# Two neighbouring tokens per partition, and the heads in two halves, in a gated-linear-attention plus feed-forward kernel

## Chip, cores, metric

The kernel runs on one core of one Trainium2 chip. The metric is device time in microseconds (us). "Span" is the length of the profiled execution as the profile shows it, 1.7 to 2.9 us shorter than the time of the same run. Runs are marked fast or slow (over 1.5% above the fastest of the same kernel); ratios use fast runs alone.

Engines: PE multiplies matrices, DVE, ACT and POOL work on vectors, and SP does nothing but issue DMAs, one after the other, in the order in which the program has them. "SPq" in the profile is SP's instruction queue.

## The reference, cut to what matters

```python
# q, k, v, alpha: (B=4, H=8, S=768, D=48) float32
for t in range(S):
    state = alpha[:, :, t, :, None] * state + einsum('bhd,bhe->bhde', k[:, :, t], v[:, :, t])
    y[:, :, t] = einsum('bhd,bhde->bhe', q[:, :, t], state)
x = y.transpose(0, 2, 1, 3).reshape(3072, 384)
g = s * relu(x @ w_in) ** 2 + b          # w_in: 384 x 2048
out = g @ w_out                          # w_out: 2048 x 384
```

One caution about "correct": the constant `b` times the column sums of `w_out` makes up nearly all of the output. With the reference's own numbers, max |out| is 0.236, and max |out - bias| is 0.0020. A correctness check on `out` therefore says little of the attention part.

## The kernel before

The 3072 tokens are 24 blocks of 128. Attention is computed block by block in chunk form: cumulative sums of log alpha on PE, exponentials on ACT, q and k scaled on DVE, q and k transposed, then k^T v, the masked q k^T, and y. Block for block, y is transposed and goes through the two feed-forward layers, called MoE here as in the parameters' names. The order of all instructions is fixed beforehand by a list scheduler inside the kernel, which is given an estimated duration for each operation (the second argument of `op`).

For each block there are four loads, the store of 128 output rows, and DMA transposes for those blocks that PE does not transpose:

```python
NIN = 9              # buffers per input tensor: loads run up to 9 blocks ahead
N_PE_T = 12          # blocks 0..11 are transposed by PE, 12..23 by DMA
...
a_in = many("a_in", NIN, [128, H, D], FP32)      # one token per partition; q_in, k_in, v_in too

def load(n, src, dst):
    b, c = n // NCH, n % NCH
    nc.sync.dma_start(
        out=dst[n % NIN],
        in_=src[b, :, c * C : (c + 1) * C, :].rearrange("h s d -> s h d"),
    )                                            # 1024 pieces of 48 floats = 192 bytes

def st_Tdma(n):                                  # q and k of a block, one DMA
    nc.sync.dma_start_transpose(
        out=qkT_sb[n % 3].rearrange("a x p t -> a (x p) t"),
        in_=qk_sb[n % 3].rearrange("a x h d -> a (x h d)"),
    )

def ostore(x):
    n = x // 4
    nc.sync.dma_start(out=out[n * C : (n + 1) * C, :], in_=out_sb[(x // 4) % NOUT])
...
op("SP", 0.45, ranks[x, n], load, n, src, dst, w=[(x, n % NIN)], lat=1.2, dma=0.98)
op("SP", 0.5, -3000, st_Tdma, n, r=[("qb", i3), ("kb", i3)], w=[("qkT", i3)], lat=TLAT, dma=1.6)
```

The bias needs column sums of `w_out`, which POOL adds up early on:

```python
def colsum_part(i):
    nc.gpsimd.tensor_tensor(out=colpart if i else colsum,
        in0=wst[i][:, 0 : QW // 2], in1=wst[i][:, QW // 2 : QW], op=ALU.add)
...
op("POOL", 1.3, -2, colsum_part, i, r=[("wst", i)], w=["colpart" if i else "colsum"])
op("PE", 1.3, -10, bias_mm, r=["bones", "colsum"], w=["bps"], lat=0.27, take=("b", 0))
```

## Time and profile before

| | before |
|---|---|
| time, median of 4 runs | 202.02 us (201.06 to 204.6; the 204.6 is a slow run) |
| span of the profiled run | 198.0 us, clock 0.974, fast |
| PE busy | 173.1 us, 87% of the span |
| DMAs issued by SP (its timeline) | 148 |
| last input load issued | 148.5 us |
| last q/k transpose issued | 151.5 us |

A table of stretches of the kernel before. The columns are the stretch, its length, busy us of PE, PEld, DVE, ACT and POOL with their instruction counts, the granted PE clock, the mean busy share of the 16 DMA engines, and GB/s:

```profile
0.00:50.00 50.00, 31.25 (x323) 23.90 (x324) 27.36 (x43) 25.30 (x52) 26.14 (x41) 0.91 1.02 217
60.00:120.00 60.00, 58.23 (x691) 39.88 (x689) 50.48 (x85) 44.56 (x106) 25.31 (x35) 1.00 0.97 192
```

Some of that seems to be back-pressure: a load issue takes from 0.37 us to over 4 us, the long ones where the DMA engines are full. How much of the 89% is the bare cost of an issue, and how much is waiting for a saturated DMA, can't be read off; only the shortest issues hint at it (0.37 to 0.44 us for a load, 1.24 us for a q/k transpose, 0.33 us for a store).

### The profile page before, as it was taken

The numbers are of one execution on the slowest core, as the hardware profiler recorded it, in microseconds if no ns is written. First come the engines' busy times: TensorE is split into PE (matmuls) and PEld (weight loads), VectorE is DVE, ScalarE is ACT, GpSimd is POOL, SyncE is SP. The second block draws the span as 40 slices with busy tenths as digits, with TensorE's granted clock in tenths as the row PEclk, the third lists the DMA queues.
The fourth block names the chain that finished last, engine by engine and source line by source line (L and its number), as shares of the span: only waits on it lengthen the run. The fifth ranks groups of instructions, "written<-read, shape, count | busy, mean of one in ns | idle before, by whom it ended". The sixth has DMA issues, their size and how long they took to land.

```text
span 198.0 us, 4422 instructions
## 1 busy us (share of the span) xinstructions
PE 173.1 (87%) x1664; PEld 111.3 (56%) x1664; DVE 130.1 (66%) x223; ACT 114.1 (58%) x249; POOL 66.2 (33%) x97
## 2 busy tenths in 40 slices
PE   0557279985999999799999999999999999999991
PEld 0445279652778877576555564555564455455650
DVE  4545626268999999988986935896664672653321
ACT  3415307993558967778767847796336661944000
POOL 6515044996823544606154333232233000000000
PEclk9999958998899999999999999999999999999999
DMA  6998999999397989899999997989997420111112
GB/s 115 193 219 173 180 322 372 197 212 206 98 218 172 218 187 209 157 219 186 238 136 201 219 191 164 217 173 192 196 184 196 100 63 4 40 40 41 69 60 75
DMA packets 124982, 32.94 MB, mean 166 GB/s; under 512 B 118304, under 2 KB 124960, under 8 KB 124960
## 3 DMA queue, kind: packets, MB, share of 16 engines
q1 hardware_dynamic: 123072, 31.08, 73.7%
q0 software_dynamic: 1600, 1.57, 5.2%
q8 instruction: 13, 0.21, 0.4%
q14 instruction: 9, 0.07, 0.1%
q10 hardware_dynamic: 288, 0.00, 0.1%
HBM read 25.17 MB, written 4.72 MB: 151 GB/s over the span
## 4 chain that ended last, share of the span: by engine, by line
PE 62%; SPq 11%; DVE 8%; POOL 6%; DMA 6%; issue 3%; ACT 1%; DVEq 0%; POOLq 0%
PE bank L531 25%; PE bank L559 24%; SPq L274 9%; DMA v_in<-in_v_dram 4%; POOL colsum L309 3%; POOL colpart L301 3%; DMA k_in<-in_k_dram 3%; PE a_ps L446 3%; PE bank L382 2%; DVE am L455 2%; PE bank L479 2%; PE bank L405 1%; DVE qk L370 1%; DVE gt L552 1%; PE bank L338 1%
## 5 line engine op out<-in xcount | busy, mean ns | idle before, releaser
L540 ACT ACTIVATE r<-bank 128x512 bf16<-128x512 f32 x96 | 56.2, 602 | 34.6 <-PE bank L531 18.1
L531 PE MATMUL bank<-xd,w_in_bf 128*128 128x128 bf16 (+2 forms) x480 | 75.2, 303 | 0.8 <-DMA w_in_bf<-in_moe_w_in_dram 0.5
L559 PE MATMUL bank<-w_out_bf,gt 128*128 128x384 bf16 x384 | 71.9, 328 | 0.6 <-ACT w_out_bf L298 0.5
L552 DVE TENSOR_TENSOR gt<-r 128x512 bf16<-128x512 bf16 x96 | 48.4, 520 | 25.3 <-ACT r L540 24.9
L531 PEld LDWEIGHTS <-w_in_bf 128*128 128x128 bf16 x480 | 39.8, 103 | 20.4 <-DMA w_in_bf<-in_moe_w_in_dram 0.7
L559 PEld LDWEIGHTS <-gt 128*128 128x128 bf16 x384 | 36.0, 98 | 25.9 <-issue 2.0
L455 DVE TENSOR_TENSOR am<-a_ps,mask 128x1024 bf16<-128x1024 f32 x24 | 29.2, 1219 | 5.1 <-PE a_ps L446 4.9
L435 POOL TENSOR_TENSOR s_st<-t,blast 64x192 bf16<-64x192 bf16 x32 | 18.5, 579 | 35.3 <-DVE t L428 14.7
L359 POOL CAST vb<-v_in 128x384 bf16<-128x384 f32 x24 | 15.4, 642 | 32.6 <-DMA v_in<-in_v_dram 26.5
L331 ACT ACTIVATE la<-a_in 128x384 bf16<-128x384 f32 x24 | 12.7, 531 | 11.7 <-DMA a_in<-in_alpha_dram 11.7
L362 DVE TENSOR_TENSOR qk<-q_in,b_s 128x384 bf16<-128x384 f32 x24 | 15.7, 656 | 4.9 <-ACT b_s L352 4.8
L370 DVE TENSOR_TENSOR qk<-k_in,binv 128x384 bf16<-128x384 f32 x24 | 15.9, 664 | 3.5 <-DMA k_in<-in_k_dram 3.5
L352 ACT ACTIVATE b_s<-bank 128x384 f32<-128x384 f32 x24 | 11.8, 492 | 9.1 <-PE bank L343 8.8
L591 POOL TENSOR_TENSOR o_sb<-o_sb,bias_w 128x384 f32<-128x384 f32 x12 | 12.5, 1043 | 12.2 <-ACT o_sb L582 9.8
L568 DVE SCALAR_TENSOR_TENSOR o_sb<-bank,s_col,bias_w 128x384 f32<-128x384 f32 x12 | 7.4, 615 | 13.6 <-PE bank L559 13.6
L492 ACT ACTIVATE yn<-bank 128x384 bf16<-128x384 f32 x24 | 11.9, 497 | 5.8 <-PE bank L479 5.6
L428 DVE TENSOR_TENSOR t<-bank,s_st 128x384 bf16<-128x384 f32 x16 | 8.8, 551 | 7.0 <-PE bank L405 5.0
L338 PE MATMUL bank<-la,U_bf 128*128 128x384 bf16 x24 | 8.2, 340 | 5.0 <-POOL bones L313 4.7
L405 PE MATMUL bank<-vb,qk 128*128 128x96 bf16 x80 | 7.3, 218 | 5.4 <-POOL vb L359 4.1
L355 ACT ACTIVATE binv<-bank 128x384 f32<-128x384 f32 x24 | 11.8, 490 | 0.0
L479 PE MATMUL bank<-vb,am 128*128 128x48 bf16 x192 | 9.0, 186 | 3.0 <-DVE am L455 2.8
L382 PE MATMUL bank<-ident_bf,qk 128*128 128x128 bf16 x96 | 9.9, 250 | 1.6 <-DVE qk L362 1.2
(44 smaller groups left out, 130.7 us busy)
## 6 DMA issues: line engine op xcount, KB each, us to landing
a_in<-in_alpha_dram SPq DMA_DIRECT2D x24, 192.0 KB, 3.6
q_in<-in_q_dram SPq DMA_DIRECT2D x24, 192.0 KB, 3.7
k_in<-in_k_dram SPq DMA_DIRECT2D x24, 192.0 KB, 3.8
v_in<-in_v_dram SPq DMA_DIRECT2D x24, 192.0 KB, 4.0
out_dram<-o_sb SPq DMA_DIRECT2D x24, 192.0 KB, 2.4
wst<-in_moe_w_out_dram SPq DMA_DIRECT2D x4, 768.0 KB, 10.1
w_in_bf<-in_moe_w_in_dram POOLq DMA_DIRECT2D x4, 384.0 KB, 7.0
qkT<-qk SPq DMA_TRANSPOSE x12, 3.6
```

Of the source, the lines that this page charges most:

```text
L274: nc.sync.dma_start(out=dst[n % NIN], in_=src[b, :, c * C : (c + 1) * C, :].rearrange("h s d -> s h d"),)
L359: nc.gpsimd.tensor_copy(out=vb_sb[n % 3], in_=v_in[n % NIN])
L362: nc.vector.tensor_tensor(out=qk_sb[n % 3][:, 0, :, 0:D], in0=q_in[n % NIN], in1=b_sb[n % 2], op=ALU.mult,)
L370: nc.vector.tensor_tensor(out=qk_sb[n % 3][:, 1, :, 0:D], in0=k_in[n % NIN], in1=binv_sb[n % 2], op=ALU.mult,)
L382: nc.tensor.transpose(out=t_ps[:, x, p, :], in_=f[:, 128 * p : 128 * p + 128], identity=ident_bf,)
L435: nc.gpsimd.tensor_tensor(out=s_sb[n % 2][rows, :, cols], in0=t1_sb[n % 2][rows, :, cols], in1=blast_sb[n % 2][rows].unsqueeze(2).to_broad ...
L455: nc.vector.tensor_tensor(out=am_sb[n % 2].rearrange("a e p t -> a (e p) t"), in0=a_ps.rearrange("a e p t -> a (e p) t"), in1=mask.unsquee ...
L479: nc.tensor.matmul(out=y_ps[:, 48 * h : 48 * h + 48], lhsT=am[:, h % 2, h // 2, :], rhs=vb[:, 48 * h : 48 * h + 48], start=(h == 0 and not ...
L531: nc.tensor.matmul(out=hp[:, i * n : (i + 1) * n], lhsT=w_in_bf[:, kk, 128 * j : 128 * (j + 1)], rhs=xd_sb[g % 3][:, kk, 0:n], start=(kk = ...
L540: nc.scalar.activation(out=r_sb[w % 2], in_=bank("h", w), func=AF.Relu)
L552: nc.vector.tensor_tensor(out=dst, in0=r, in1=r, op=ALU.mult)
L559: nc.tensor.matmul(out=op[:, 0:d_model], lhsT=gt_sb[:, slot, j, :], rhs=w_out_bf[:, j, :], start=(j == 0), stop=(j == NJ - 1),)
```

## The change

The intent: each partition holds two neighbouring tokens of four heads, instead of one token of eight heads. Two neighbouring tokens of one head are contiguous in memory, so the transfers become 384 bytes instead of 192, which should take less DMA time for the same data. Partitions 0 to 63 hold heads 0 to 3, and 64 to 127 hold heads 4 to 7; even and odd tokens are two "slots" in the free dimension. Everything else follows: cumulative sums take three matmuls, q k^T sixteen 64x64 quadrants instead of eight half-array matmuls, and v is stored block-diagonally (zeros elsewhere) so that both halves go through one matmul. As the two halves lie in different partitions and different heads, each load, each q/k transpose and each store becomes two DMAs of half the size.

The change also moves other things: PE transposes q and k only of blocks 0 to 2 instead of 0 to 11, so nine more blocks use DMA transposes; column sums go from POOL to DVE; dummy matmuls keep the PE clock up in the first 36 us; ACT issues half of the loads of blocks 0 to 2. The order of the first loads, the grouping of blocks for the feed-forward layers and the split of the output work between engines change as well.

The diff, cut to its core:

```diff
-NIN = 9
-N_PE_T = 12
+NIN = 8
+N_PE_T = 3
+N_PE_Y = 12
+N_ACT_LOAD = 3
...
-    a_in = many("a_in", NIN, [128, H, D], FP32)
+    a_in = many("a_in", NIN, [128, G, 2, D], FP32)         # G = H // 2
...
-    def load(n, src, dst):
+    def load(eng, n, src, dst, e):
         b, c = n // NCH, n % NCH
-        nc.sync.dma_start(
-            out=dst[n % NIN],
-            in_=src[b, :, c * C : (c + 1) * C, :].rearrange("h s d -> s h d"),
-        )
+        eng.dma_start(                                     # R = C // 2 = 64
+            out=dst[n % NIN][R * e : R * e + R].rearrange("i h t d -> i h (t d)"),
+            in_=src[b, G * e : G * e + G, c * C : (c + 1) * C, :].rearrange(
+                "h (i t) d -> i h (t d)", t=2
+            ),
+        )
...
     def st_Tdma(n):
-        nc.sync.dma_start_transpose(
-            out=qkT_sb[n % 3].rearrange("a x p t -> a (x p) t"),
-            in_=qk_sb[n % 3].rearrange("a x h d -> a (x h d)"),
-        )
+        for g in range(2):
+            nc.sync.dma_start_transpose(
+                out=qkT_sb[n % 3][:, g].rearrange("a x u c -> a (x u) c"),
+                in_=qk_sb[n % 3][R * g : R * g + R].rearrange("a x u e d -> a (x u e d)"),
+            )
...
     def st_A(n):
         qkT = qkT_sb[n % 3]
-        for p in range(NP):
-            for e in range(2):
-                nc.tensor.matmul(
-                    out=a_ps[:, e, p, :],
-                    lhsT=qkT[64 * e : 64 * e + 64, 1, p, :],
-                    rhs=qkT[64 * e : 64 * e + 64, 0, p, :], ...)
+        for t in range(2):
+            for p in range(2):
+                for g in range(2):
+                    for e in range(2):
+                        nc.tensor.matmul(
+                            out=a_ps[R * g : R * g + R, e, p, t, :],
+                            lhsT=qkT[64 * e : 64 * e + 64, g, 1, 2 * t + p],
+                            rhs=qkT[64 * e : 64 * e + 64, g, 0, 2 * p : 2 * p + 2], ...)
...
     def ostore(x):
-        nc.sync.dma_start(out=out[n * C : (n + 1) * C, :], in_=out_sb[(x // 4) % NOUT])
+        for t in range(2):
+            nc.sync.dma_start(
+                out=out[n * C : (n + 1) * C, :].rearrange("(j t) m -> t j m", t=2)[t],
+                in_=out_sb[(x // 4) % NOUT][R * t : R * t + R],
+            )
...
-            op("SP", 0.45, ranks[x, n], load, n, src, dst, w=[(x, n % NIN)], lat=1.2, dma=0.98)
+            for e in range(2):
+                eng = nc.scalar if e and n < N_ACT_LOAD else nc.sync
+                op("ACT" if eng is nc.scalar else "SP", 0.45, ranks[x, n], load, eng, n, src, dst, e,
+                   w=[(x, n % NIN, e)], lat=1.2, dma=0.34)
```

## The prediction

> **What bounds it now.** The table of stretches of time shows PE busy 97 to 100% from 50 to 180 us; the chain of waits gives PE 62% of the span. So the kernel is PE-bound after a bad first 50 us, in which PE did about 24 us of useful work, counted at the warm spacing of its timeline: 13 first-layer and 9 second-layer units at 0.66 us, attention for about 4 blocks, the 2.1 us fp32 bias. The other 26 us are waits and cold clock: 4.7 us before the first matmul; 4.1 us until v of block 2 lands (DMA share about 1 from 5 to 35 us); granted clock 0.50 from 25 to 30 us; 3.0 us waiting for the column sums on POOL (adds of 1.85 us). After 50 us only 3 to 4 us are lost; the tail after the last matmul is 4 us.
>
> **PE work** (warm start-to-start, timeline). Before, per block: cumulative sum 0.27, transposes 0.44 (12 blocks), k^T v 0.17, q k^T 0.33, y 0.47, y transpose 0.17 (12 blocks). After, estimates from the same spacings: sum 0.43 (two more 192-column matmuls), k^T v 0.33 (192 columns for 96), q k^T about 0.5 (sixteen 64x64 quadrants for eight), y 0.54. Transposes on PE fall to 3 blocks (-4.0 us), the bias halves (-1.1). Sum: 164 us before, about 172 after: +8 us on the bounding engine. Least certain is q k^T: the Trainium skill, "TensorEngine Tiling (Array Packing)", Restrictions, says column tiling disables fast weight load; the trace has only 128-column loads (95 ns).
>
> **DMA.** 192-byte packets move 196 GB/s when saturated (15.7 ns a packet on each of 16 engines), 1536-byte ones about 350 (70 ns). A line through both puts 384 bytes at 23 ns: 0.75 us a tensor instead of 1.0. The Trainium skill, "DMA: Bandwidth & Descriptors", Specifications, puts line rate at 512 B and up: a gain, not a doubling. It saves 24 us of DMA in all, 4 us in the first 16 tensors; nine more blocks transposed by DMA spend most of it. After 50 us DMA is not the bound. SP issues twice as many loads; its queue gets fuller (about 150 us), a risk.
>
> **Start.** Twelve load issues stand before the first Ln on ACT (about 0.5 us each), and the POOL prelude grows from 4.7 to about 9 us. So the first Ln comes near 8 us, not 4.2, the first MoE matmul near 17, not 14. But then blocks 1, 2 and 3 are there, dummy matmuls hold the clock, and column sums on DVE don't stop PE: from about 20 us it runs nearly full. Loss before steady state: 14 to 17 us instead of 26.
>
> **Sum.** -10 us at the start, +8 us PE work: a tie by this count; it charges the small matmuls fully, so I lean to a gain: 196.5 us, range 189 to 204. Faster by over 2%: 0.52; within: 0.37; slower: 0.11.
>
> **What would show it.** First MoE matmul at 16 to 18 us; no PE idle over 2 us after 22 us; granted clock 1.0 from 20 us; useful PE work in the first 50 us up from 24 to about 35 us; loads near 290 GB/s when saturated; q k^T 0.45 to 0.6 us a block; PE 97% or more to the end.
>
> **What would break it.** Quadrant matmuls at 0.8 us a block; half-size DMA transposes costing as much as whole ones, or the SP queue, starving attention after 60 us; DVE overloaded at 30 to 50 us by column sums; w_in late because POOL issues it late.

## More of the kernel before

The page of the kernel before: busy time of the engines; then the span in 40 slices of 4.95 us each, with the busy share in tenths (9 is 90% or more); then the chain of work that ended last.

```profile
span 198.0 us, 4422 instructions
PE 173.1 (87%) x1664; PEld 111.3 (56%) x1664; DVE 130.1 (66%) x223; ACT 114.1 (58%) x249; POOL 66.2 (33%) x97
...
PE   0557279985999999799999999999999999999991
...
PEclk9999958998899999999999999999999999999999
DMA  6998999999397989899999997989997420111112
...
PE 62%; SPq 11%; DVE 8%; POOL 6%; DMA 6%; issue 3%; ACT 1%; DVEq 0%; POOLq 0%
```

From about 50 us on (slice 10) PE is at 9 nearly everywhere, and it makes up 62% of the chain. The losses lie in the first slices. But the DMA row stands at 7 to 9 nearly everywhere too, up to slice 30, so two resources run near full side by side.

The timeline of SP in the kernel before; the columns are start, duration, line, and what is issued. L274 is a load, L395 a q/k transpose, L511 a y transpose, L579 a store:

```profile
99.94 0.57 SPq L274 DMA_DIRECT2D a_in<-in_alpha_dram  x1
100.60 1.21 SPq L511 DMA_TRANSPOSE xd<-yn  x1
101.86 0.57 SPq L274 DMA_DIRECT2D q_in<-in_q_dram  x1
...
103.17 2.57 SPq L395 DMA_TRANSPOSE qkT<-qk  x1
105.84 0.53 SPq L579 DMA_DIRECT2D out_dram<-o_sb  x1
```

These durations are the time for which SP is held by one issue.

Between 60 and 148.5 us SP is issuing for 79.2 of 88.5 us, 89%.

## The result, and the profile after

The changed kernel takes 279.93 us (median of 4, 278.48 to 280.57), against 202.02 us before. All its runs are fast ones; of the four before, the 204.6 us run is a slow one and left out of the ratio. The ratio is 1.387, with a 95% interval of 1.377 to 1.397. (A ratio here is the mean time of one kernel's fast runs over that of the other's of the same rounds, so not quite the ratio of the medians quoted beside it.) The prediction, 196.5 us with a range up to 204, was wrong by 83 us.

The page of the kernel after; the slices are now 6.97 us long:

```profile
span 278.8 us, 5424 instructions
PE 208.3 (75%) x2025; PEld 139.9 (50%) x2025; DVE 130.8 (47%) x255; ACT 112.1 (40%) x243; POOL 61.8 (22%) x128
...
PE   4188899295766868496859649749669868999993
...
PEclk9997999868995979777995995986887997999999
DMA  5999976566656666557656668656656556220132
...
PE 36%; DMA 25%; SPq 25%; ACT 4%; issue 3%; DVE 3%; POOL 1%; ACTq 0%; DVEq 0%; POOLq 0%
```

Up to slice 4 (35 us) DMA is full, and PE is busy from slice 2 on (of its work in these 35 us, 6.0 us are the dummy matmuls). After that PE is at 4 to 9, once at 2, with no pattern, for 200 us, and it is not the DMA engines that fill up in its place: they fall from 9 to 5 to 7. In the chain PE's share went from 62 to 36%; SP's queue went from 11 to 25%, and DMA from 6 to 25%.

The same stretches of the kernel after, to set beside those of before:

```profile
0.00:50.00 50.00, 35.95 (x497) 30.00 (x498) 30.82 (x60) 25.47 (x54) 21.45 (x59) 0.97 0.89 202
60.00:120.00 60.00, 40.92 (x497) 30.66 (x496) 26.20 (x49) 23.95 (x58) 16.82 (x26) 0.84 0.63 129
```

From 60 to 120 us PE is busy for 40.9 us instead of 58.2, at a granted clock of 0.84, and DMA moves 129 GB/s at a share of 0.63 instead of 192 at 0.97. What PE waits for is shown by the waits of the kernel after (who waits for what: us in total, times, longest):

```profile
POOL vb L436 <- DMA v_in<-in_v_dram: 93.9, 24, 9.8
ACT la L394 <- DMA a_in<-in_alpha_dram: 64.9, 19, 5.8
...
PE bank L401 <- ACT la L394: 29.6, 16, 6.5
```

The cumulative sums on PE (L401) wait for Ln on ACT (the longest such wait, 6.5 us, is the late start; 17.1 of the 29.6 us fall between 60 and 223 us), and Ln waits 64.9 us in total for alpha to land; before it was 11.7 us. So the inputs come late, although DMA engines are free. The timeline of SP tells why. L325 is a load, L477 a q/k transpose, L669 a store; "x2" is two issues in a row:

```profile
98.78 1.28 SPq L325 DMA_DIRECT2D k_in<-in_k_dram  x2
100.11 1.27 SPq L325 DMA_DIRECT2D v_in<-in_v_dram  x2
101.49 2.54 SPq L477 DMA_TRANSPOSE qkT<-qk  x2
104.12 1.26 SPq L325 DMA_DIRECT2D a_in<-in_alpha_dram  x2
...
106.14 1.20 SPq L669 DMA_DIRECT2D out_dram<-o_sb  x2
```

SP issues almost without a gap (0.05 us between issues). A half load holds it for 0.59 us at least, 0.61 us typically. Here that is hardly back-pressure, since the DMA share is 0.6; and the very first half load of this kernel, with nothing in flight yet, took 0.76 us. A half-size q/k transpose holds it 1.2 us, as long as a whole one did (1.24 us at least before), and a half store 0.58 us. From 60 to 223 us SP is issuing for 149.5 of 163 us, 92%, and the rest is nearly all gaps of under 0.2 us between issues. It issues 286 DMAs instead of 148, and over the whole run its issues take 218 us instead of 145; the last load goes out at 223.7 us instead of 148.5, the last q/k transpose at 234.7 instead of 151.5. The 92% alone would prove nothing, as it was 89% before, with back-pressure in it; what tells is the DMA share beside it, 0.63 here and 0.97 before. The load stream has a ceiling that can be worked out (an estimate): 98,304 bytes per issue of 0.61 us and a gap of 0.05 us is 149 GB/s. In a stretch in which SP issued nothing but loads, the table of the kernel after shows 138 GB/s at a DMA share of 0.62:

```profile
38.00:47.00 9.00, 8.57 (x107) 6.16 (x106) 7.48 (x14) 7.46 (x17) 1.12 (x2) 1.00 0.62 138
```

**Theory.** SP's issue rate is the bound. Cutting each DMA in two nearly doubled the number of issues (18 of the 138 more are the q/k transposes of nine more blocks), and a half does not cost half. Per block that is about 8 x 0.61 + 2 x 1.22 + 2 x 0.58 us, and 1.2 us more for the y transpose of twelve blocks: 8.5 to 9.7 us, while PE needs about 7 us for a block (an estimate: 168 us over 24 blocks, counted at the warm spacings of its timeline).

**Rivals.** (a) The DMA engines handle the 384-byte packets, or the many DMAs, badly. (b) The half-size transposes alone are to blame. (c) The late start: the first MoE matmul comes at 26.5 us instead of 14.0, since ACT issues twelve loads ahead of its first Ln. (d) PE's new matmuls are slow, quadrants above all.

### The profile page after: what moved, and what is told of

It is laid out like the page before. It is cut to its first block, busy times and chain, and to the rows that moved or that the text cites. A ratio compares the mean times of both kernels' runs of the same rounds, so it can differ in the third digit from the quotient of the medians.

```text
span 278.8 us, 5424 instructions
## 1 busy us (share of the span) xinstructions
PE 208.3 (75%) x2025; PEld 139.9 (50%) x2025; DVE 130.8 (47%) x255; ACT 112.1 (40%) x243; POOL 61.8 (22%) x128
## 4 chain that ended last, share of the span: by engine, by line
PE 36%; DMA 25%; SPq 25%; ACT 4%; issue 3%; DVE 3%; POOL 1%; ACTq 0%; DVEq 0%; POOLq 0%
SPq L325 16%; PE bank L620 15%; DMA a_in<-in_alpha_dram 13%; PE bank L648 12%; SPq L477 5%; DMA k_in<-in_k_dram 5%; SPq L669 4%; DMA q_in<-in_q_dram 3%; DMA v_in<-in_v_dram 3%; PE bank L568 2%; ACT la L394 2%; PE bank L401 2%; ACT r L629 1%; PE bank L488 1%; DVE am L540 1%
## 5 line engine op out<-in xcount | busy, mean ns | idle before, releaser
L620 PE MATMUL bank<-xd,w_in_bf 128*128 128x128 bf16 (+2 forms) x576 | 83.1, 296 | 1.3 <-ACT r L629 1.3
L648 PE MATMUL bank<-w_out_bf,gt 128*128 128x384 bf16 x384 | 80.4, 354 | 0.1
L620 PEld LDWEIGHTS <-w_in_bf 128*128 128x128 bf16 x576 | 48.6, 106 | 23.6 <-issue 8.0
L436 POOL CAST vb<-v_in 64x384 bf16<-64x384 f32 x48 | 26.5, 553 | 116.8 <-DMA v_in<-in_v_dram 93.9
L394 ACT ACTIVATE la<-a_in 128x384 bf16<-128x384 f32 x24 | 12.5, 526 | 75.4 <-DMA a_in<-in_alpha_dram 64.9
L444 DVE TENSOR_TENSOR qk<-q_in,b_s 128x192 bf16<-128x192 f32 x48 | 17.5, 406 | 37.6 <-ACT b_s L422 24.3
L401 PE MATMUL bank<-la,U_bf 128*128 128x384 bf16 x24 | 9.5, 395 | 29.6 <-ACT la L394 29.6
L518 POOL TENSOR_TENSOR s_st<-t,blast 64x192 bf16<-64x192 bf16 x32 | 17.6, 549 | 32.5 <-PE bank L557 11.7
L488 PE MATMUL bank<-vb,qk 128*128 128x192 bf16 x80 | 11.6, 275 | 17.4 <-POOL vb L436 17.3
L568 PE MATMUL bank<-vb,am 128*128 128x96 bf16 x192 | 14.8, 231 | 7.9 <-DVE am L540 7.9
L488 PEld LDWEIGHTS <-qk 128*128 128x128 bf16 x80 | 7.6, 108 | 20.3 <-issue 15.3
L568 PEld LDWEIGHTS <-am 128*128 128x128 bf16 x192 | 12.0, 113 | 9.1 <-DVE am L540 8.3
L531 PE MATMUL a_ps<-qkT 64*64 64x128 bf16 x384 | 11.6, 233 | 4.7 <-DMA qkT<-qk 4.6
```

Source lines behind the costliest of these rows:

```text
L394: nc.scalar.activation(out=la_sb[n % 2][:, :, :, 0:D], in_=tokens(a_in[n % NIN]), func=AF.Ln)
L436: nc.gpsimd.tensor_copy(out=vb_sb[n % 3][rows, :, e].rearrange("a t (h d) -> a t h d", h=G), in_=tokens(v_in[n % NIN][rows]),)
L444: nc.vector.tensor_tensor(out=qk_sb[n % 3][:, 0, heads, :, 0:D], in0=tokens(q_in[n % NIN][:, heads]), in1=b_sb[n % 2][:, :, heads], op=ALU ...
L488: nc.tensor.matmul(out=p_ps[:, p], lhsT=kb[:, 2 * t + p], rhs=vb[:, t, :, 96 * p : 96 * p + 96], start=(t == 0), stop=(t == 1),)
L518: nc.gpsimd.tensor_tensor(out=s_sb[n % 2][rows, :, cols], in0=t1_sb[n % 2][rows, :, cols], in1=blast_sb[n % 2][rows].unsqueeze(2).to_broad ...
L568: nc.tensor.matmul(out=y_ps[:, :, 48 * h : 48 * h + 48], lhsT=am[:, e, p, t, :], rhs=vb[:, t, :, 48 * h : 48 * h + 48], start=(h == 0 and ...
```

## The experiments

Thirteen kernels were run. "Ratio" is against the kernel before in the same rounds; its median was between 198.5 and 199.9 us in all of them.

| run | made from | edit | median us | ratio |
|---|---|---|---|---|
| e1_whole_issues | after | one DMA instead of two, everywhere | 209.38 | 1.051 |
| e2_T_on_PE | after | all transposes of q, k on PE | 245.68 | 1.237 |
| e3_loads_two_queues | after | second halves of all loads issued by ACT | 265.47 | 1.335 |
| e4_before_half_loads | before | each load in two DMAs of 64 partitions | 237.52 | 1.195 |
| e5_whole_loads_only | after | one DMA per load only | 228.42 | 1.150 |
| e6_loads_two_queues_late | after | second halves on ACT, not those of blocks 3 to 7 | 259.84 | 1.309 |
| e7_before_colsum_DVE | before | column sums on DVE | 194.25 | 0.981 |
| e8_no_loads_on_ACT | after | no loads on ACT | 283.06 | 1.429 |
| e9_before_loads_by_heads | before | each load in two DMAs of 128 partitions | 217.87 | 1.094 |
| e10_T_on_PE_two_queues | after | e2 and e6 together | 232.57 | 1.171 |
| e11_colsum_and_T_by_DMA | before | e7, and nine more blocks transposed by DMA | 210.21 | 1.060 |
| e12_colsum_and_v2_earlier | before | e7, and other order of first loads | 198.70 | 1.000 |
| e13_late_queue_clean_start | after | e2, and second halves on ACT from block 12 on | 242.35 | 1.215 |

### e1_whole_issues: the changed kernel with whole DMAs

The bytes and the 384-byte packets stay, but each pair of DMAs is one. With the two halves holding different heads, no single DMA could be found that puts the data where the kernel wants it; so this kernel loads, transposes and stores *wrong data* (same amounts, same shapes of packets). Its output is wrong, which doesn't matter for the time.

```diff
 def load(eng, n, src, dst, e):
+    if e: return
+    s0 = min(c * C, S - 2 * C)
-        out=dst[n % NIN][R * e : R * e + R]..., in_=src[b, G * e : G * e + G, c * C : (c + 1) * C, :]...
+        out=dst[n % NIN]..., in_=src[b, 0:G, s0 : s0 + 2 * C, :]...        # 128 partitions, heads 0..3
 # q/k transpose: one of 128 partitions instead of two of 64; store: one of 128 rows; no loads on ACT
```

> The changed kernel with the same bytes, the same 384-byte packets and the same work on every engine, but one issue where it has two: one 128-partition load per tensor and block, one transpose, one store, all on SP. Data are wrong on purpose (each load takes 256 tokens of four heads). Theory SP (the changed kernel is bound by the SP queue, which takes 0.6 us for each half load, 1.22 us for each half transpose, 0.58 us for each half store, about 9.2 us a block): with about 4.5 us a block SP is no longer the limit, the PE is: 195 to 210 us. Rival DMA (the transfers themselves, smaller destination halves or the transposes, are the limit): bytes and packets are the same, so 260 us or more. Rival PE (quadrant matmuls, cold clock): unchanged, 270 to 280 us.

Measured: 209.38 us (207.24 to 211.8), ratio 1.051. That is inside the expected range. The profiled run is the slow one (211.8 us), so its durations and DMA rates are read, not its span. The timeline of SP in e1, where L328 is a load:

```profile
100.97 0.43 SPq L328 DMA_DIRECT2D k_in<-in_k_dram  x1
101.45 0.58 SPq L328 DMA_DIRECT2D v_in<-in_v_dram  x1
...
103.22 0.45 SPq L668 DMA_DIRECT2D out_dram<-o_sb  x1
```

And the same stretches of the table in e1:

```profile
38.00:47.00 9.00, 9.00 (x121) 6.97 (x120) 8.85 (x17) 8.32 (x19) 4.84 (x6) 1.00 1.08 285
60.00:120.00 60.00, 53.77 (x649) 39.01 (x652) 43.63 (x86) 38.73 (x91) 22.41 (x39) 0.91 1.08 233
```

Twice the bytes now go out in about 0.5 us of SP, and the last load is issued at 120.4 us instead of 223.7. 285 GB/s in place of 138 from 38 to 47 us, with the same packets and the same matmuls: that refutes (d) as the cause of the 80 us, and (a) as far as the packets go. Nor do the many DMAs clog the engines: from issue to landing a load took a median of 2.9 to 3.0 us in the kernel after, and 3.6 to 4.0 before. The change cost 38.7% (ratio 1.387); with whole DMAs it costs 5.1%. So 33.6 of the 38.7 points, about 67 us, go with the second issues. Not quite all of it need be theirs: e1 also has no loads on ACT, and its first MoE matmul comes at 19.6 us instead of 26.5, so up to 7 us may be the earlier start. The other 5 points, some 10 us, stay: by the same table DMA is saturated (1.08) from 60 to 120 us, where the loads end, and PE is not full until then. So even with half the issues this change would not have won.

### e5_whole_loads_only: only the loads made whole

e1's edit of the loads alone, again with wrong data.

```diff
 def load(eng, n, src, dst, e):        # as in e1
 # q/k transposes and stores stay in halves
```

> As e1_whole_issues, but only the loads are whole; transposes and stores stay two half issues each. Data wrong on purpose. Theory SP, by addition: the stores and transposes cost 1.2 + 2.5 us a block on SP as before the experiment, the loads 2 us instead of 5.2: about 6 to 7 us a block, near the PE's 7: 212 to 228 us, between e1_whole_issues (209.4) and the changed kernel (280). If the half transposes were the cause and the loads not, it stays above 255.

Measured: 228.42 us (226.88 to 230.41), ratio 1.150, 0.4 us above what was expected. So 23.7 points (1.387 - 1.150, about 47 us, with the same earlier start in it) go with the second issue of each load, and 9.9 points (1.150 - 1.051, about 20 us) with the second transposes and stores. Rival (b) fails: the transposes are the smaller part.

### e4_before_half_loads: the kernel before, with nothing changed but the cut of its loads

The counter-proof, with right data and without any other part of the change.

```diff
 def load(n, src, dst):
-    nc.sync.dma_start(out=dst[n % NIN], in_=src[b, :, c * C : (c + 1) * C, :].rearrange("h s d -> s h d"))
+    for e in range(2):
+        nc.sync.dma_start(
+            out=dst[n % NIN][64 * e : 64 * e + 64],
+            in_=src[b, :, c * C + 64 * e : c * C + 64 * e + 64, :].rearrange("h s d -> s h d"))
```

> The kernel before with each load issued as two loads of 64 partitions on SP; same 192-byte packets, same bytes, right result. Theory SP: eight issues of 0.6 to 0.65 us a block, 5.2 us, plus 1.3 to 3 us of transposes and stores: loads are late and the time rises to 215 to 235 us. Rival DMA or PE: bytes and packets are the same, 200 to 206 us.

Measured: 237.52 us (235.65 to 238.34), ratio 1.195, 2.5 us above the expected range and far from the 200 to 206 us of the rivals. The same 192-byte packets, the same bytes, the same work of PE: 39 us slower for being asked for in two. The timeline of SP in e4:

```profile
0.72 1.52 SPq L275 DMA_DIRECT2D a_in<-in_alpha_dram  x2
...
99.57 1.27 SPq L275 DMA_DIRECT2D a_in<-in_alpha_dram  x2
100.94 1.27 SPq L275 DMA_DIRECT2D q_in<-in_q_dram  x2
102.31 1.27 SPq L275 DMA_DIRECT2D k_in<-in_k_dram  x2
```

Again 0.63 us for each half, with a DMA share of 0.78 from 60 to 120 us. The last load goes out at 188.7 us instead of 148.5, 40.2 us later, and the span grows by 37.7 us. This carries the theory without the wrong data of e1. It agrees with a rule that could have been looked up: the Trainium skill, "DMA: Bandwidth & Descriptors", Rules for kernel authors, says of two transfers to disjoint partition halves "Don't bother" and to use one 128-partition transfer. Its reason is that the halves share the same DMA engines. Here the larger harm is that the second issue costs SP as much as the first.

### e9_before_loads_by_heads: two DMAs of 128 partitions

The same number of issues as e4 (244), but cut along the heads, so that each DMA still covers 128 partitions.

```diff
+    for e in range(2):
+        nc.sync.dma_start(
+            out=dst[n % NIN][:, 4 * e : 4 * e + 4],
+            in_=src[b, 4 * e : 4 * e + 4, c * C : (c + 1) * C, :].rearrange("h s d -> s h d"))
```

> The kernel before with each load issued as two loads of all 128 partitions and four heads each; packets, bytes and number of issues are those of e4_before_half_loads (237.5 us), only the cut is along the heads instead of the partitions. If an issue costs by its count alone, 0.6 us each, this is as slow as e4: 230 to 240 us. If the 64-partition cut makes each issue dearer (0.60 us at least in e4, 0.37 to 0.45 for 128 partitions in the kernel before), a load issue here takes 0.40 to 0.50 us and the time is 204 to 220 us.

Measured: 217.87 us (215.2 to 218.16), ratio 1.094. The timeline of SP in e9:

```profile
0.73 1.00 SPq L275 DMA_DIRECT2D a_in<-in_alpha_dram  x2
...
101.86 1.05 SPq L275 DMA_DIRECT2D v_in<-in_v_dram  x2
103.01 1.01 SPq L275 DMA_DIRECT2D a_in<-in_alpha_dram  x2
```

A half load costs 0.50 to 0.53 us here, against 0.63 in e4, and with as many issues the kernel is some 20 us faster (217.87 against 237.52). So it is not the count alone: a load to 64 partitions holds SP longer than one of the same bytes to 128. Back-pressure does not explain it: the first load of the program, with nothing in flight yet, holds SP for 0.73 us in e4 and for 0.45 us in e9 (the second for 0.73 and 0.49). Why that is so, no run shows.

### e8_no_loads_on_ACT: the late start

```diff
-N_ACT_LOAD = 3
+N_ACT_LOAD = 0
```

> The changed kernel with no load issued from ACT: SP issues all. The twelve issues on ACT held the first Ln until 12.5 us. Without them the first Ln should begin at 3.5 to 5 us and the first MoE matmul at 19 to 22 us instead of 26.5. SP gets 12 more issues (7.5 us). Theory SP: the end is set by SP's total, so no gain or a loss: 278 to 290 us. If the late start were a main cause of the loss: 265 us or less.

Measured: 283.06 us (281.68 to 284.67), ratio 1.429. The first MoE matmul now comes at 17.7 us, nearly 9 us earlier than in the changed kernel, and yet the kernel is no faster; SP has twelve more issues. Rival (c) fails as the cause of the end time: what is won at the start is lost while waiting for SP.

### e2, e3, e6, e10, e13: five attempts to get below SP's limit with right data

All five take issues away from SP in the changed kernel. All five came out slower than expected, by 5 to 25 us beyond the range. By the words put down beforehand, e3 (265.47 us) even falls just inside the range of its rival, one limit behind both queues (265 to 285), and e13 (242.35 us) into what would speak against SP (232 or more). The traces say otherwise, see below.

e2 does every q/k transpose on PE (42 DMA issues fewer):

```diff
-N_PE_T = 3
+N_PE_T = 24
```

> The changed kernel with q and k transposed on PE in all 24 blocks, no DMA transpose of them. Theory SP: 42 issues of 1.27 us leave the SP queue, 53 us: 220 to 235 us, with SP still the limit at about 6.5 us a block. Rival DMA transposes (their transfers, not their issues, are the limit): below 210 us at once, with SP no longer full. Rival PE: slower than 280 us, as PE gets 9 us more work.

Measured: 245.68 us (244.35 to 246.58). It won 34 us. Loads, y transposes and stores still keep SP issuing for 90% of the time from 60 us to the last load at 158.9 us; from 180 us on PE is full. The direction agrees with the theory, the size was missed by at least 10 us.

e3 lets ACT, which has a DMA queue too, issue the second half of every load:

```diff
-N_ACT_LOAD = 3
+N_ACT_LOAD = 24
```

> The changed kernel with the second half of every load issued from ACT instead of SP (before: only of the first three blocks). Theory SP: 84 issues of 0.65 us leave SP, 55 us; ACT takes them on: 220 to 240 us. Rival DMA (one shared resource behind both queues, transfers or descriptor generation): unchanged, 265 to 285 us. Rival PE: unchanged.

Measured: 265.47 us (262.78 to 265.77). A flawed experiment: the fixed order put the loads of all eight buffers ahead of ACT's first activations, and PE was busy for 0.49 us between 20 and 40 us. e6 keeps blocks 3 to 7 off ACT:

```diff
-eng = nc.scalar if e and n < N_ACT_LOAD else nc.sync
+eng = nc.scalar if e and (n < N_ACT_LOAD or n >= 8) else nc.sync
```

> e3_loads_two_queues without its flaw (there ACT issued the loads of all eight buffers before its first Ln, which then began after 40 us): second halves go to ACT for blocks 0 to 2 as in the changed kernel, and again from block 8 on, where they wait for buffers and so are spread out; blocks 3 to 7 are on SP alone. Theory SP: 64 issues of 0.65 us leave SP, 42 us; e2 got back 34 of 53 us: 240 to 255 us. Rival (one limit behind both queues): 272 us or more.

Measured: 259.84 us (258.39 to 262.44). Its first MoE matmul comes at 35.2 us, 9 us later than in the changed kernel; so it does in e10 (34.8 us). e10 is e2 and e6 together:

```diff
-N_PE_T = 3
+N_PE_T = 24
-eng = nc.scalar if e and n < N_ACT_LOAD else nc.sync
+eng = nc.scalar if e and (n < N_ACT_LOAD or n >= 8) else nc.sync
```

> e2 and e6 together: the changed kernel with all q and k transposes on PE and the second halves of the loads of blocks 0 to 2 and from 8 on issued from ACT. Theory SP: 95 us of issues leave the SP queue, about 4.5 us a block remain, under the PE's 7: SP stops being the limit; PE has 9 us more work than in the changed kernel and the start is as late as there: 208 to 224 us. If something else than the SP queue kept it at 260 in e6, it stays above 235.

Measured: 232.57 us (231.37 to 235.48), the fastest of this layout with right data, but above the expected range. In e13 the start is free of ACT's loads; they begin with block 12:

```diff
-N_PE_T = 3
+N_PE_T = 24
-eng = nc.scalar if e and n < N_ACT_LOAD else nc.sync
+eng = nc.scalar if e and n >= 12 else nc.sync
```

> e10_T_on_PE_two_queues with a clean start: no load on ACT before block 12 (as e8, first MoE matmul at 18 to 20 us), second halves of blocks 12 to 23 on ACT, all q and k transposes on PE; right result. Theory SP: 90 us of issues leave SP. SP still gets eight issues of 0.65 us a block until block 11, about 6.5 us a block with stores, then half of that. The last load should be issued by 125 to 140 us and the time be 212 to 226 us. If SP were not what held e10 and e2, it stays at 232 or more.

Measured: 242.35 us (241.04 to 243.74). The timeline of ACT in e13 shows what goes wrong in this family; in brackets is how long ACT did no computing and what it waited for last:

```profile
48.74 0.22 ACT L431 ACTIVATE blast<-bank 128x4 bf16<-128x4 f32 x1
52.99 0.63 ACTq L325 DMA_DIRECT2D v_in<-in_v_dram  x1
53.73 0.62 ACTq L325 DMA_DIRECT2D q_in<-in_q_dram  x1
54.45 0.60 ACTq L325 DMA_DIRECT2D k_in<-in_k_dram  x1
...
56.61 0.52 ACT L394 ACTIVATE la<-a_in 128x384 bf16<-128x384 f32 x1 [7.65 <-DMA q_in<-in_q_dram]
```

ACT runs its instructions in order. A load that must wait for its buffer (until 52.99 us here, when POOL has read the old data) stands in front of the next Ln, which starts as soon as the last of five issues is out, and each issue takes 0.6 us from ACT too. One limit behind both queues does not show: in e10, 47 of SP's loads went out mostly while ACT was issuing one, and took a median of 0.61 us, the same as the 43 that did not overlap. And in e13 PE is busy for 28.3 of the 30 us from 90 to 120 us and stays near full to the end; the time was lost before that, with 17.7 of 30 us from 60 to 90. So the five say less about SP's limit than they were meant to: they exchange it for a stalled ACT. The theory rests on e1, e4, e5 and e9. A version of the changed layout with right results and clear of SP's limit was not reached.

### e7, e11, e12: a part of the change that pays, on the kernel before

e7 moves only the column sums to DVE, later in the order, as the change does:

```diff
-op("POOL", 1.3, -2, colsum_part, ...)       # and colsum_add; nc.gpsimd in both
+op("DVE", 1.0, 30.0, colsum_part, ...)      # nc.vector in both
-op("PE", 1.3, -10, bias_mm, ...)
+op("PE", 1.3, 30.0, bias_mm, ...)
```

> The kernel before with only one part of the change: column sums of w_out on DVE at a low priority instead of POOL, and the bias matmul at the same low priority. If the 3.0 us for which PE waited for POOL at 44 to 47 us, and the drained pipeline after it, were a loss as I predicted: 3 to 6 us faster, 193 to 196 us beside 199. If DVE, busy 98% from 60 to 80 us, is disturbed by them: within 1% of before.

Measured: 194.25 us (193.36 to 196.24), ratio 0.981, interval 0.976 to 0.987. This is the fastest kernel. The gain is just under 2%, but the interval excludes no change. The timeline of PE in the kernel before:

```profile
42.50 1.47 PE L531 MATMUL bank<-xd,w_in_bf 128*128 128x256 bf16 x12
46.99 2.14 PE L319 MATMUL bank<-colsum,bones 128*128 128x384 f32 x4 [3.02 <-POOL colsum L309]
```

and in e7, without the wait of 3.0 us:

```profile
44.79 0.82 PE L559 MATMUL bank<-w_out_bf,gt 128*128 128x384 bf16 x4
45.45 1.45 PE L319 MATMUL bank<-colsum,bones 128*128 128x384 f32 x4
```

e11 adds the change's smaller N_PE_T to e7, with whole transposes:

```diff
 # e7, and for the q/k transpose
-if n < N_PE_T:
+if n < 3:
```

> e7_before_colsum_DVE (194.3 us) plus a second part of the change on the old layout: q and k transposed by DMA from block 3 on, one whole transpose a block. PE loses 4.0 us of transposes, DVE 6 us of copies; SP gains 9 issues of 1.2 us and up. If PE is the limit: 189 to 193 us. If DMA (share already about 1.0 from 0 to 140 us) or SP is at its edge: 195 us or more.

Measured: 210.21 us (209.49 to 211.57), ratio 1.060, 16 us slower than e7. The DMA share is about 0.9 to 1.1 up to 160 us there. So nine more blocks on DMA transposes are a loss by themselves in the kernel before, most likely as its full DMA engines have nothing to spare. The prediction had taken them as nearly free.

e12 adds to e7 only another order of the first loads, to end the wait for v of block 2:

```diff
-LOADS = '... a2 q2 k2 a3 q3 k3 v2 v3 ...'
+LOADS = '... a2 q2 k2 v2 a3 q3 k3 v3 ...'
```

> e7_before_colsum_DVE plus v of block 2 and 3 loaded in their turn instead of after block 3: the wait of PE for v of block 2 (2.3 us in e7, with a cold clock after it) should go: 1 to 4 us faster than e7, 190 to 193 us, unless a wait for q or k of block 3 takes its place: within 1 us of e7.

Measured: 198.70 us (196.47 to 199.3), ratio 1.000: both expectations missed, some 4 us slower than e7. In its trace the wait for v of block 2 is gone, as intended, and the first MoE matmul comes at 13.9 us (13.4 in e7). The loss comes later: from 40 to 60 us PE is busy for 17.4 us, against 18.9 in e7, and after 50 us its waits add up to 6.4 us, against 2.9. The new order of loads changed the order of much else; which part of it costs the time stays open.

## Why the prediction was wrong, point by point

**The step that failed** is this one: "After 50 us DMA is not the bound. SP issues twice as many loads; its queue gets fuller (about 150 us), a risk". The doubled loads were seen, and the SP queue and the price of half-size transposes even stood in the list of what would break it, but the size of the queue was wrong and it was left out of the sum. SP's issues took 218 us, not 150; they had taken 145 us in the kernel before, back-pressure included, so that 150 leaves next to nothing for twice as many. How it was counted, the prediction does not say. The runs show 0.61 us for a half load (e4: 0.63, without the rest of the change), 1.2 us for a half-size transpose as for a whole one, and 0.58 us for a half store. What was put down as +0 us was nearly the whole result: issuing whole DMAs gives back 33.6 of 38.7 points (e1), 23.7 of them by the loads (e5).

There was a deeper fault: the queue was taken as one more total to compare with the span, and 150 us of 196 looked harmless. But the stream has to end early. In before, after, e4 and e9 the span ends 44 to 47 us after the last q/k transpose is issued (198.0 - 151.5, 278.8 - 234.7, 235.7 - 191.5, 216.1 - 171.4), as all of the last blocks' feed-forward work comes after it. SP's loads and q/k transposes thus had about 150 us, not 196 (an estimate: 196 less 46). At the durations of the kernel after, these alone come to about 161 us (180 x 0.61 and 42 x 1.22 us, an estimate), before y transposes, stores and gaps.

**DMA not the bound after 50 us**: true of the kernel after only because SP kept the engines at 0.6. As soon as SP is relieved (e1) they saturate, with a share of 1.08 from 60 to 120 us, and e11 shows the nine more transposed blocks costing 16 us in the kernel before, where DMA was full already. The prediction called these transposes a thing that "spends most of" the saving, and then priced it at nothing.

**384-byte transfers, about 290 GB/s when saturated**: right, and not seen in the kernel after, where issuing allows about 149. In e1 the stretch from 38 to 47 us shows 285 GB/s, nearly all of it in 384-byte packets at 23.0 ns each, the figure that the prediction had. That also fits the source that the prediction named, the Trainium skill, "DMA: Bandwidth & Descriptors", Specifications: a gain below 512 bytes, not yet line rate.

**PE work +8 us**: no worse than that, by the parts that were measured. The timeline of PE in the kernel after, warm:

```profile
42.29 0.42 PE L531 MATMUL a_ps<-qkT 64*64 64x128 bf16 x16
42.64 0.34 PE L401 MATMUL bank<-la,U_bf 128*128 128x384 bf16 x1
...
43.08 0.83 PE L620 MATMUL bank<-xd,w_in_bf 128*128 128x128 bf16 x12
```

Sixteen quadrants take 0.35 us (42.29 to 42.64), not 0.5; eight half-array matmuls took 0.33 before. The cumulative sum takes 0.44 us (predicted 0.43), k^T v 0.33 (0.33). The prediction had named the Trainium skill, "TensorEngine Tiling (Array Packing)", Restrictions, for the loss of fast weight load under column tiling. The weight loads do show something of the kind, a median of 107 ns for the 64x64 loads of q k^T, against 94 for the 64x128 ones before, but they overlap so far that it costs next to nothing here. That column tiling is the reason was not tested.

**Start**: first Ln at 12.5 us (predicted 8), first MoE matmul at 26.5 (predicted 17). ACT's twelve issues took 0.60 to 0.83 us each instead of the estimated 0.5, and between them ACT waited another 2.5 us, mostly for earlier loads to land; POOL issued w_in in pieces up to 19.5 us, as the list of risks had it. The POOL prelude of about 9 us was right (9.6). So the 10 us that the start was to win did not come: without the dummy matmuls PE was busy for about 30 of the first 50 us, against 31.2 before. This step failed too, but it did not decide the end time (e8).

**PE full and clock at 1.0 from 20 us on**: wrong as a consequence. PE starves, and the granted clock falls to 0.84 from 60 to 120 us. The Trainium skill, "TensorE: Matmul & The Clock Gate", What's actually happening, says that an idle window of about 3.4 us takes the array back to half clock. The trace agrees in direction only: PE has gaps of up to 5.3 us after 40 us, and half clock follows them, but PE need not be idle for a whole window. Each of the twelve stretches at half clock that begin between 50 and 235 us comes after 3.4 us in which PE was still busy for 0.15 to 1.67 us. This adds to the loss, but it is an effect of the starving and not its cause.

**Column sums on DVE don't stop PE**: right, and by itself worth 1.9% on the kernel before (e7).

**Open**: why a load to 64 partitions holds SP for 0.61 us and one of the same bytes to 128 partitions for about 0.5; where exactly e1's last 10 us go (saturated DMA, more PE work and a start at 19.6 us instead of 14.0 are all there, and were not separated); e12; and a version of this layout with right results and few issues.

## What to carry to other kernels

A queue that issues DMAs is an engine with its own busy time: count its issues, multiply by the shortest durations in the trace (of the same kind, and to as many partitions), and compare the sum with the time by which the last input must have left, not with the span. Halving a DMA did not halve the issue in any run here; so bytes per issue divided by time per issue is a bandwidth ceiling, to be set beside that of the packets before a layout is cut in two. When a layout gains on packet size but needs a second DMA per tensor, cut along an axis that keeps all partitions in each DMA (e9 against e4), and first make sure that the queue has room; moving issues to a computing engine's in-order queue is no free room.

## What the Trainium skill lacked or had wrong

- "DMA: Bandwidth & Descriptors", Issuing engines are not separate DMA queues, says that the time a sequencer takes to initiate a DMA "is usually small relative to the DMA itself". For one DMA that holds here too: 0.61 us of a median 2.9 us from issue to landing. But issues come one after the other and transfers overlap, so the issues were the bound: 0.61 us and a gap of 0.05 us for a 96 KB load are a ceiling of about 149 GB/s (an estimate), where the DMA engines moved 285 GB/s with the same packets in e1.
- The same page has no table of issue times in us for trn2 (cycles per instruction stand only in its part on trn3). This case shows, for DMAs issued from SP: loads to 128 partitions 0.37 us at least and about 0.5 typically in e1 and e9; loads to 64 partitions 0.59 us at least, 0.61 to 0.63 typically; q/k transposes 1.2 us at least, whole or half; stores 0.33 us at least for 128 rows; for 64, 0.47 us at least and 0.58 us typically. ACT took 0.60 to 0.83 us for a half load in the kernel after.
- The same page's rule on partition halves ("Don't bother") is right, and gives shared DMA engines as its reason. The runs show another, which weighed more here: the second issue costs SP as much as the first, and each costs more than a 128-partition one (e4 is 39 us slower than before, e9 19 us).
- "TensorEngine Tiling (Array Packing)", Restrictions, says that column tiling disables fast weight load, without a size. In this case: 107 ns for a 64x64 weight load against 94 for a 64x128 one (that the tiling is the reason was not tested), and 0.35 us for sixteen 64x64 quadrants against 0.33 us for eight 64x128 matmuls.
- "TensorE: Matmul & The Clock Gate", What's actually happening, puts half clock "after ≥1 idle window (~3.4µs)". Here PE need not be idle for that long: half clock followed 3.4 us with up to 1.67 us of PE work in them.
